# Attention and a gated convolution on one core: keys of later batches by plain loads, every eighth probability tile turned by TensorE, and a new order of the steps

## The chip, the cores and the metric

The kernel runs on one core of a Trainium2 chip. A core has five instruction streams that run beside each other: TensorE (PE in the profile, with its weight loads as PEld), VectorE (DVE), ScalarE (ACT), GpSimd (POOL) and SyncE (SP), which here only issues DMAs. Sixteen DMA engines move the data of all queues. The metric is the device time in microseconds, as the median over runs. Beside the runs there is one profiled execution, whose trace and page are read here.

## The reference

There are four batches (B = 4) with 12288 queries of 128 channels each and a key map of 384 x 32 positions. The map is averaged over 4 x 4 blocks, which leaves 768 keys per batch; keys and values are the same matrix.

```python
kv_pool = kv.reshape(B, H//4, 4, W//4, 4, C).mean(axis=(2, 4))
k = v = kv_pool.reshape(B, -1, C) @ w_sr             # 768 keys
s = (q @ k.transpose(0, 2, 1)) / sqrt(C)
a = exp(s - s.max(-1)); a /= a.sum(-1) + 1e-9
x = a @ v                                             # attention
gate_pre[t] = sum(conv_w[k] * x[t - 4 + k] for k in range(5))   # causal, by channel
out = (sigmoid(gate_pre) * (x @ w_val)) @ w_out
```

All of it is in float32. The kernel keeps that precision by splitting operands into a high and a low part.

## The kernel before

**Tiles and groups.** Queries are taken in groups of 512 (`GQ`), 24 groups per batch, 96 in all. A group has four tiles of 128 queries (`NT = 4`), and a tile is one step of the main loop (L481). So a group is four steps, j = 0 to 3.

**One tile.** TensorE makes the 128 x 768 scores in PSUM with six matmuls (`score`, L256: high times high, high times low, low times high, for two halves of the keys). VectorE takes the row maximum (`row_max`, nm), ScalarE the exponential with its row sum (`expo`, L280), in place in PSUM. ScalarE then writes the high float16 part of the probabilities (`p_hi`, L327) and VectorE the low part (`p_lo`, L331), both into the tile `hl`. Three PSUM buffers hold scores, so the scores of a tile can be made only when `p_lo` of the tile three before is done.

**Turning the probabilities.** The product with the values needs keys on the partitions. With `NX = 4`, `on_pe` is never true: each pair of tiles is turned by one DMA transpose from `hl` to `pt` (L335), two per group, issued on SP.

**One group further.** The 18 matmuls of `av_part` (L344) read all four tiles of `pt`; they are spread over the steps of the group two later, six, three, three and six (`AV_CUTS`). The row sums are inverted, turned by a small TensorE matmul (`norm_turn`, L290), stored to DRAM (`rd`) and loaded back as one row for all partitions (`rb`). VectorE multiplies av, a column scale and `rb` to x (`g_x`, L361). For the convolution GpSimd copies four columns from the x before (L357), makes four products (`tap`, L371), then four sums (L380); ScalarE makes the fifth product (L369). Then come a tanh on ScalarE, `g_val` (L400), `g_h` on VectorE (L405), `g_out` (L410), and `g_evac` (L420) to the output tile. `g_qh` (ScalarE) and `g_ql` (GpSimd, L248) split the queries of the group two ahead.

**Keys.** The first batch's keys come before the main loop in 16 pieces of 384 KB on SP (`load_kv`, L118), each summed over 4 x 4 by VectorE (L123). The keys of each later batch come during the batch before, by `setup_steps`, one entry per group: for each half of the keys one plain load (L131, SP) and three loads that add onto it as they arrive (`accum_op`, L133, on GpSimd's queue). VectorE then sums only over the remaining four neighbours, in four instructions of 768 elements per partition (L138). After that come the projection, the split and the values.

**What sets the order.** The order is written by hand (`manual_schedule`): each engine runs its instructions as the loop emits them, and waits come from the tiles. One PSUM bank (`misc`) serves `norm_turn`, `g_val`, `g_out` and the set-up matmuls in turn.

Of the kernel before, what the change touches and what calls it, by code (L numbers as in the profile page):

```python
# [27 lines left out]
def attn_moe_kernel(ctx, tc, qT, kvT, w_sr, w_moe, outT):  # L28
# [12 lines left out]
    AV_CUTS = (0, 6, 9, 12, 18)  # L41
    assert 3 * NCH == AV_CUTS[-1]
    PC = NK // PIECES
    QC = NK // 4
# [3 lines left out]
    kvp = ctx.enter_context(tc.tile_pool(name="kvp", bufs=4))  # L48
# [3 lines left out]
    pfp = ctx.enter_context(tc.tile_pool(name="pfp", bufs=3))  # L52
# [21 lines left out]
    def load_moe():  # L74
# [4 lines left out]
        raw = kvp.tile([C, HALF * R], F32, name="rows0", bufs=1).bitcast(I32)[:, :2 * NW]  # L79
        rest = kvp.tile([C, HALF * R], F32, name="rows1", bufs=1)  # L80
# [34 lines left out]
    def load_kv(st, i):  # L115
        t = kvp.tile([C, R, PC * R], F32, name="kvt", bufs=5)
        src = kvT[0].rearrange("r c x -> c r x")
        nc.sync.dma_start(out=t, in_=src[:, :, i * PC * R:(i + 1) * PC * R])  # L118
        st["kv", i] = t

    def pool_kv(st, i):
        t = st.pop(("kv", i))
        nc.vector.tensor_reduce(out=st["pool"][:, i * PC:(i + 1) * PC],  # L123
                                in_=t.rearrange("c r (k s) -> c k r s", s=R),
                                axis=AX.XY, op=ALU.add)

    def load_rows(b, st, h, r):
        src = kvT[b, r, :, h * HALF * R:(h + 1) * HALF * R]
        if r == 0:
            st["rows", h] = kvp.tile([C, HALF * R], F32, name=f"rows{h}", bufs=1)  # L130
            nc.sync.dma_start(out=st["rows", h], in_=src)  # L131
        else:
            nc.gpsimd.dma_start(out=st["rows", h], in_=src, accum_op=ALU.add)  # L133

    def pool_rows(st, i):
        t = st["rows", i // 2].rearrange("c (k s) -> c k s", s=R)
        k0 = i % 2 * QC
        nc.vector.tensor_reduce(out=st["pool"][:, i * QC:(i + 1) * QC], in_=t[:, k0:k0 + QC],  # L138
                                axis=AX.X, op=ALU.add)
# [72 lines left out]
    def value_steps(st):  # L212
        return [lambda: trickle.extend(column_scale(st)), lambda: None, lambda: None,
                lambda: values(st, 0, misc()) or split_values(st, 0),
                lambda: values(st, 1, misc()) or split_values(st, 1)]

    def setup_steps(b, st):
# [53 lines left out]
    def on_pe(j):  # L271

        return j >= NX
# [207 lines left out]
    for t in range(NT * G):  # L481
# [16 lines left out]
        if avg:  # L498
            av_part(avg, j)
# [130 lines left out]
```

## Time and profile before

| what | value |
|---|---|
| median of 3 runs | 1246.01 us (1245.61 to 1255.13) |
| profiled execution, span of its trace | 1239.7 us |
| PE, DVE, ACT, POOL busy | 1039.8, 892.6, 899.1, 878.3 us |
| weight loads (PEld) | 674.5 us |
| DMA | 253.21 MB, mean 204 GB/s |
| DMA transposes | 192, 6.1 us from issue to landing (median) |
| loads that add (GpSimd's queue) | 18 of 768 KB, 14.5 us to landing (median) |

The page gives the profiled execution's own time as its span, 1239.7 us; the median of the timed runs is 6.3 us above it. Busy shares are means over the whole span, and no engine but the DMA is above 84% by them. So the places where the engines wait, and for whom, say more than the shares.

### The profile page before, as it was taken

Reading aid. Unit: us, or ns where it says so; the run is one execution under the profiler, and the core shown is the slowest. Engines: PE = TensorE matmul, PEld = TensorE weight load, DVE = VectorE, ACT = ScalarE, POOL = GpSimd, SP = SyncE. Lnnn points to the kernel's source line nnn. Section 1 sums busy time; section 2 is a strip of 40 time slices with the busy share of each in tenths; the row PEclk is TensorE's granted clock in tenths of the full one; section 3 lists DMA queues with packets and bytes.
Section 4 is the critical chain, followed back from the end, with each engine's and each line's share of the span. In section 5 each row is a group of like instructions: output and inputs, shape, how many; then the busy total and the mean of one; then the engine's idle time right before and its main releaser. Section 6 shows DMA issues by size and latency. Waiting matters only on the chain.

```text
span 1239.7 us, 15458 instructions
## 1 busy us (share of the span) xinstructions
PE 1039.8 (84%) x4598; PEld 674.5 (54%) x4598; DVE 892.6 (72%) x1254; ACT 899.1 (73%) x1659; POOL 878.3 (71%) x966
## 2 busy tenths in 40 slices
PE   2888778699998768779999778769999999899996
PEld 1655445466565445445666545446566666566663
DVE  6966656588886657568888556557888888787784
ACT  1867666588887557668888657656888888788882
POOL 1277667678886668667888667657788888788782
PEclk9989889899999888889999988888999999999998
DMA  7799999999999999999999999999999999999994
GB/s 248 146 217 179 218 192 214 177 213 204 211 219 209 215 174 216 194 182 225 211 225 232 172 192 218 181 169 217 222 211 217 217 213 226 203 230 212 208 221 119
DMA packets 637235, 253.21 MB, mean 204 GB/s; under 512 B 600160, under 2 KB 609120, under 8 KB 637152
## 3 DMA queue, kind: packets, MB, share of 16 engines
q1 hardware_dynamic: 634560, 238.07, 94.8%
q0 software_dynamic: 2592, 14.16, 8.6%
q8 instruction: 37, 0.61, 0.2%
q14 instruction: 46, 0.38, 0.1%
HBM read 75.83 MB, written 25.36 MB: 82 GB/s over the span
## 4 chain that ended last, share of the span: by engine, by line
PE 43%; DMA 28%; DVE 13%; ACT 9%; issue 5%; POOL 1%; SPq 0%; DVEq 0%; ACTq 0%; POOLq 0%
DMA pt<-hl 23%; PE av L344 17%; PE s L262 16%; PE m L400 5%; ACT s L280 4%; DVE nm L268 4%; PE m L410 3%; DVE x L361 3%; DMA rb<-rd 3%; DVE hl L331 3%; ACT hl L327 2%; DMA kvt<-in_kv 1%; DMA q<-in_q 1%; DVE h L405 1%; ACT th L396 1%
## 5 line engine op out<-in xcount | busy, mean ns | idle before, releaser
L344 PE MATMUL av<-pt,vh 128*128 128x512 f16 x1140 | 420.2, 397 | 134.1 <-DMA pt<-hl 102.5
L280 ACT ACTIVATE s<-s,nm 128x768 f32<-128x768 f32 x384 | 335.6, 874 | 257.5 <-DVE z L287 146.4
L331 DVE SCALAR_TENSOR_TENSOR hl<-s,hl 128x768 f16<-128x768 f32 x384 | 363.0, 945 | 25.1 <-ACT hl L327 24.8
L380 POOL TENSOR_TENSOR sum<-sum,tap 128x512 f32<-128x512 f32 x282 | 359.9, 1276 | 26.4 <-ACT tap L369 4.4
L268 DVE TENSOR_REDUCE nm<-s 128x1 f32<-128x768 f32 x384 | 364.3, 949 | 2.6 <-PE s L262 2.6
L371 POOL TENSOR_SCALAR tap<-x,wm 128x512 f32<-128x512 f32 x376 | 253.6, 696 | 149.2 <-DVE x L361 146.9
L327 ACT ACTIVATE hl<-s 128x768 f16<-128x768 f32 x384 | 310.6, 809 | 18.4 <-issue 6.6
L344 PEld LDWEIGHTS <-vh 128*128 128x128 f16 x1164 | 116.5, 100 | 315.2 <-issue 192.2
L262 PE MATMUL s<-kh,qh 128*128 128x384 f32 x768 | 267.0, 430 | 21.2 <-DVE hl L331 15.5
L248 POOL TENSOR_TENSOR ql<-q,qh 128x512 fp32r<-128x512 f32 x96 | 121.6, 1267 | 163.8 <-ACT qh L244 154.1
L344 PE MATMUL av<-pt,vl 128*128 128x512 f16 x570 | 226.2, 397 | 0.0
L262 PE MATMUL s<-kl,qh 128*128 128x384 f32 x768 | 201.6, 344 | 0.0
L361 DVE SCALAR_TENSOR_TENSOR x<-av,down,rb 128x512 f32<-128x512 f32 x95 | 71.3, 751 | 180.1 <-DMA rb<-rd 89.8
L262 PE MATMUL s<-kh,ql 128*128 128x384 f32 x768 | 200.3, 342 | 0.0
L262 PEld LDWEIGHTS s<-kh,qh 128*128 128x128 f32 x768 | 142.9, 199 | 85.3 <-PE m L290 28.0
L262 PEld LDWEIGHTS s<-kl,qh 128*128 128x128 f32 x768 | 144.6, 195 | 0.5 <-DVE kl L163 0.5
L262 PEld LDWEIGHTS s<-kh,ql 128*128 128x128 f32 x768 | 143.3, 193 | 0.0
L380 POOL TENSOR_TENSOR sum<-tap,tap 128x512 f32<-128x512 f32 x94 | 119.8, 1275 | 0.0
L405 DVE SCALAR_TENSOR_TENSOR h<-th,m 128x512 f32<-128x512 f32 x94 | 64.7, 688 | 68.0 <-PE m L400 51.7
L344 PEld LDWEIGHTS <-vl 128*128 128x128 f16 x582 | 58.2, 100 | 88.4 <-issue 67.7
L400 PE MATMUL m<-x,wm 128*128 128x512 f32 x188 | 100.0, 614 | 5.5 <-DVE r L297 5.5
L410 PE MATMUL m<-h,wm 128*128 128x512 f32 x188 | 96.9, 596 | 3.9 <-DVE h L405 3.9
(62 smaller groups left out, 639.9 us busy)
## 6 DMA issues: line engine op xcount, KB each, us to landing
rb<-rd SPq DMA_DIRECT2D x96, 256.0 KB, 3.7
q<-in_q SPq DMA_DIRECT2D x47, 512.0 KB, 5.6
out<-o SPq DMA_DIRECT2D x46, 512.0 KB, 3.8
rows<-in_kv POOLq DMA_DIRECT2D x18, 768.0 KB, 14.5
kvt<-in_kv SPq DMA_DIRECT2D x16, 384.0 KB, 5.7
rows<-in_kv SPq DMA_DIRECT2D x6, 768.0 KB
pt<-hl SPq DMA_TRANSPOSE x192, 6.1
rd<-r SPq DMA_DIRECT2D x96, 2.0 KB
```

Of the source, the lines that this page charges most:

```text
L248: nc.gpsimd.tensor_tensor(out=g.ql, in0=g.q, in1=g.qh.bitcast(F32), op=ALU.subtract)
L262: nc.tensor.matmul(s[:, h, :HALF], a[:, sl], k[:, h * HALF:(h + 1) * HALF], start=(i == 0), stop=(i == 2))
L268: nc.vector.tensor_reduce(out=nm, in_=g.s[j], axis=AX.XY, op=ALU.max, negate=True)
L280: nc.scalar.activation(out=halves(g.pf[j]) if on_pe(j) else g.s[j], in_=g.s[j], func=AF.Exp, bias=g.nm.pop(j), accum_out=g.z[:, j:j + 1])
L327: nc.scalar.activation(out=part(g, j, 0), in_=g.s[j], func=AF.Copy, scale=2.0 ** 15)
L331: nc.vector.scalar_tensor_tensor(out=part(g, j, 1), in0=g.s.pop(j), scalar=2.0 ** 15, in1=part(g, j, 0), op0=ALU.mult, op1=ALU.subtract)
L344: nc.tensor.matmul(out, g.st[v][:, k * P:(k + 1) * P], g.pt[:, j0:j1, a * NCH + k], start=(i == 0), stop=(i == len(AV_ORDER) - 1))
L361: nc.vector.scalar_tensor_tensor(out=g.x[:, HALO + c0:HALO + c1], in0=av, scalar=g.st["down"], in1=g.rb[:, c0:c1], op0=ALU.mult, op1=ALU.mult)
L371: eng.tensor_scalar(out=g.tap[k], in0=src, scalar1=w, scalar2=1.0, op0=ALU.mult, op1=ALU.mult)
L380: nc.gpsimd.tensor_tensor(out=s, in0=acc, in1=g.tap[k], op=ALU.add)
L400: nc.tensor.matmul(m, wval, g.x[:, HALO + c0:HALO + c1], start=True, stop=True)
L410: nc.tensor.matmul(m, wout, h, start=True, stop=True)
```

## The change

**Keys of later batches.** The loads that add are gone. Each later batch comes in eight plain loads of 768 KB on SP, two pieces each, one in every second group (k = 1, 3, ... 15 of the batch), into three buffers. VectorE sums all 16 pieces, one per group, at step j = 1 of the groups k = 3 to 18, with the instruction that the first batch used (L123). Projection, split and values are placed at j = 1 of fixed groups (11, 19, 22, 23).

**Turning.** In every second group (odd index) the last tile, j = 3, is turned by six TensorE transposes: `expo` writes it to SBUF (`pf`), TensorE turns it back into its own PSUM buffer between the last three av matmuls, and `p_hi` and `p_lo` write it straight into `pt`. Its neighbour j = 2 goes alone through a DMA transpose of half the size. All other tiles go as before.

**Order.** x, with the convolution behind it, moves from the end of j = 3 to the end of j = 0 of the next group; the last sum of the convolution moves behind ScalarE's product at j = 1. `g_out` and `g_evac` move to j = 0 one group later, `g_val` to j = 2, `g_h` to j = 3. `norm_turn` uses spare columns of a score buffer instead of the `misc` bank. `g_qh` and `g_ql` move to j = 3. The av matmuls are spread three, six, three, six. Queries are loaded four groups ahead (three buffers) instead of two.

**Beginning and end.** The first batch's keys come in two single pieces, six double pieces and two single pieces, three loads ahead; the first queries are split late in that phase; the last weights are loaded after it. The tail is rearranged to fit.

```diff
-    AV_CUTS = (0, 6, 9, 12, 18)
+    AV_CUTS = (0, 3, 9, 12, 18)
...
-    def load_rows(b, st, h, r):
-        src = kvT[b, r, :, h * HALF * R:(h + 1) * HALF * R]
-        if r == 0:
-            st["rows", h] = kvp.tile([C, HALF * R], F32, name=f"rows{h}", bufs=1)
-            nc.sync.dma_start(out=st["rows", h], in_=src)
-        else:
-            nc.gpsimd.dma_start(out=st["rows", h], in_=src, accum_op=ALU.add)
...
+    def load_kv(b, st, i, n=2):
+        t = kvp.tile([C, R, 2 * PC * R], F32, name="kvt")[:, :, :n * PC * R]
+        src = kvT[b].rearrange("r c x -> c r x")
+        nc.sync.dma_start(out=t, in_=src[:, :, i * PC * R:(i + n) * PC * R])
...
+    def setup_step(k, b, st):
+        if k == 1:
+            key_tiles(st)
+        if k < PIECES and k % 2 == 1:
+            load_kv(b, st, k - 1)
+        if 3 <= k < 3 + PIECES:
+            pool_kv(st, k - 3)
+        if k == 20:
+            trickle.extend(column_scale(st))
...
-    def on_pe(j):
-        return j >= NX
+    def on_pe(g, j):
+        return g.i % 2 == 1 and j == NT - 1
...
+    def turn(g, j, k):
+        c = k % (NCH // 2) * P
+        nc.tensor.transpose(g.s[j][:, k // (NCH // 2), c:c + P],
+                            g.pf[j][:, k * P:(k + 1) * P], ident)
...
-        if j % 2:
-            j0 = j - 1
+        if on_pe(g, j):
+            return
+        if j % 2 or on_pe(g, j + 1):
+            j0 = j - j % 2
             nc.sync.dma_start_transpose(
...
         if nxt:
             score(nxt, (j + 1) % NT)
-        if mg and j == 1:
+        if last and j == 1:
+            norm_turn(last, nxt.spare)
+        if og and j == 0:
+            og.m = g_out(og.h, misc())
...
+        if avg:
+            av_slice(avg, lo, mid)
+        if mg and j == 2:
             mg.m = g_val(mg, misc())
...
+        if turned:
+            for i in range(NCH):
+                turn(cur, j, i)
+                if avg and mid + i < hi:
+                    av_slice(avg, mid + i, mid + i + 1)
+            cur.pf.pop(j)
+        else:
+            p_hi(cur, j)
...
+        if turned:
+            p_hi(cur, j)
         if prev:
             p_lo(prev, (j - 1) % NT)
...
-        if avg and j == 3:
-            new_x(avg, xg, nc.gpsimd.tensor_copy)
-            g_x(avg, avg.av)
-        if xg and j == 1:
-            g_conv(xg)
+        if xg and j == 0:
+            new_x(xg, mg, nc.gpsimd.tensor_copy)
+            g_x(xg, xg.av)
+            g_conv(xg)
+        if mg and j == 3:
+            mg.h = g_h(mg.th, mg.m)
+        if ahead is not None and j == 1:
+            setup_step(k, cur.b + 1, ahead)
```

**TensorE, at the end of step j = 3 of a group, and of an odd group now.** Before, the last four of that step's six av matmuls, with their weight loads, are followed by the next tile's scores (s).

```order
L344 LDWEIGHTS vh
L344 MATMUL av<-pt,vh 128x512
L344 LDWEIGHTS vh
L344 MATMUL av<-pt,vh 128x512
L344 LDWEIGHTS vl
L344 MATMUL av<-pt,vl 128x512
L344 LDWEIGHTS vh
L344 MATMUL av<-pt,vh 128x512
L262 MATMUL s<-kh,qh 128x384 x2
```

Now the last three av matmuls alternate with the transposes of `pf` (L302), and three more transposes stand ahead of the next scores.

```order
L302 MATMUL s<-ident,pf 128x128
L338 LDWEIGHTS vh
L338 MATMUL av<-pt,vh 128x512
L302 MATMUL s<-ident,pf 128x128
L338 LDWEIGHTS vl
L338 MATMUL av<-pt,vl 128x512
L302 MATMUL s<-ident,pf 128x128
L338 LDWEIGHTS vh
L338 MATMUL av<-pt,vh 128x512
L302 MATMUL s<-ident,pf 128x128 x3
L256 MATMUL s<-kh,qh 128x384 x2
```

So the first transpose waits for ScalarE's exponential of that tile, and three av matmuls and the next scores stand behind it on TensorE.

**VectorE, one group in the main loop, from x to the step before the next x.** Before, nm is the row maximum, hl the low part, r the turned row sums, h the gated values.

```order
L361 SCALAR_TENSOR_TENSOR x<-av,down,rb 128x512
L268 TENSOR_REDUCE nm<-s 128x1
L287 RECIPROCAL z_102<-z_102 128x4
L331 SCALAR_TENSOR_TENSOR hl<-s,hl 128x768
L268 TENSOR_REDUCE nm<-s 128x1
L297 COPY r<-m 4x128
L331 SCALAR_TENSOR_TENSOR hl<-s,hl 128x768
L405 SCALAR_TENSOR_TENSOR h<-th,m 128x512
L268 TENSOR_REDUCE nm<-s 128x1
L331 SCALAR_TENSOR_TENSOR hl<-s,hl 128x768
L268 TENSOR_REDUCE nm<-s 128x1
L331 SCALAR_TENSOR_TENSOR hl<-s,hl 128x768
```

Now a group with a piece of keys to sum (pool from kvt) stands so.

```order
L355 SCALAR_TENSOR_TENSOR x<-av,down,rb 128x512
L263 TENSOR_REDUCE nm<-s 128x1
L323 SCALAR_TENSOR_TENSOR hl<-s,hl 128x768
L123 TENSOR_REDUCE pool<-kvt 128x48
L292 COPY r<-s 4x128
L263 TENSOR_REDUCE nm<-s 128x1
L323 SCALAR_TENSOR_TENSOR hl<-s,hl 128x768
L263 TENSOR_REDUCE nm<-s 128x1
L323 SCALAR_TENSOR_TENSOR hl<-s,hl 128x768
L404 SCALAR_TENSOR_TENSOR h<-th,m 128x512
L263 TENSOR_REDUCE nm<-s 128x1
L282 RECIPROCAL z_102<-z_102 128x4
```

The reciprocal and one low part now stand ahead of x, h stands two tiles later, and the sum over keys stands behind the first low part, with the copy of r behind it.

**SP, two groups while keys of the next batch arrive.** Before, the loads that add are on GpSimd's queue and SP has four transposes of 24 blocks in two groups.

```order
L298 DMA rd<-r 4x128
L335 DMA_TRANSPOSE pt<-hl 128x24x128
L303 DMA rb<-rd 128x512
L335 DMA_TRANSPOSE pt<-hl 128x24x128
L298 DMA rd<-r 4x128
L335 DMA_TRANSPOSE pt<-hl 128x24x128
L303 DMA rb<-rd 128x512
L233 DMA q<-in_q 128x1024
L335 DMA_TRANSPOSE pt<-hl 128x24x128
L424 DMA out<-o 128x1024
```

Now one of the four transposes has 12 blocks, and the load of keys stands among them.

```order
L293 DMA rd<-r 4x128
L329 DMA_TRANSPOSE pt<-hl 128x24x128
L298 DMA rb<-rd 128x512
L329 DMA_TRANSPOSE pt<-hl 128x24x128
L118 DMA kvt<-in_kv 128x4x384
L293 DMA rd<-r 4x128
L329 DMA_TRANSPOSE pt<-hl 128x24x128
L329 DMA_TRANSPOSE pt<-hl 128x12x128
L298 DMA rb<-rd 128x512
L227 DMA q<-in_q 128x1024
```

The key load stands ahead of the odd group's row sums and transposes, and the half transpose follows the whole one directly.

More of the change, by code (lines that the diff above doesn't have):

```diff
@@ L264, in score @@
         g.s[j] = s[:, :, :HALF]
+        g.spare = s[:, 0, HALF:]
     def row_max(g, j):
@@ L372, in tap, with add_taps @@
                               op0=ALU.mult, op1=ALU.mult)
+    def add_taps(g, acc, k):
+        s = work.tile([C, GQ], F32, name=f"sum{1 - k % 2}", bufs=1 if k % 2 else 2)
+        nc.gpsimd.tensor_tensor(out=s, in0=acc, in1=g.tap[k], op=ALU.add)
+        return s
     def g_conv(g):
@@ L376, in g_conv, with g_conv_last @@
             tap(g, k, nc.gpsimd)
-        acc = g.tap[0]
-        for i, k in enumerate(range(1, TAPS)):
-            s = work.tile([C, GQ], F32, name=f"sum{i % 2}", bufs=1 + i % 2)
-            nc.gpsimd.tensor_tensor(out=s, in0=acc, in1=g.tap[k], op=ALU.add)
-            acc = s
-        g.gate = acc
+        g.gate = g.tap[0]
+        for k in range(1, TAPS - 1):
+            g.gate = add_taps(g, g.gate, k)
+    def g_conv_last(g):
+        g.gate = add_taps(g, g.gate, TAPS - 1)
     def conv_dve(g, c0=0, c1=GQ):
@@ L492, in attn_moe_kernel @@
         if nxt:
             score(nxt, (j + 1) % NT)
-        if mg and j == 1:
-            mg.m = g_val(mg, misc())
+        if last and j == 1:
+            norm_turn(last, nxt.spare)
+        if og and j == 0:
+            og.m = g_out(og.h, misc())
+        if gi == 1 and j in (0, 1):
+            values(st, j, misc())
+            high, low = split_values(st, j)
+        if ahead is not None and j == 1 and k > 1:
+            high, low = setup_matmul(k, ahead)
+        turned = on_pe(cur, j)
@@ new lines, in attn_moe_kernel @@
+        lo, hi = AV_CUTS[j], AV_CUTS[j + 1]
+        mid = lo + 3 if turned else hi
+        if avg:
+            av_slice(avg, lo, mid)
+        if mg and j == 2:
+            mg.m = g_val(mg, misc())
+        if last and j == 2:
+            norm_store(last)
+        row_max(cur, j)
+        if last and j == 0:
+            norm_reciprocal(last)
+        expo(cur, j)
+        if turned:
[4 more added lines that the diff above has]
+            cur.pf.pop(j)
+        else:
+            p_hi(cur, j)
@@ L496, in attn_moe_kernel @@
+        if j == NT - 1:
+            norm_eps(cur)
+            if at(gi + 2):
+                g_qh(at(gi + 2))
+        if og and j == 0:
+            out_tile(og)
+            g_evac(og, og.m)
+        if xg and j == 1:
+            tap(xg, TAPS - 1, nc.scalar)
+            g_conv_last(xg)
         if mg and j == 2:
-            mg.m = g_out(mg.h, misc())
-        if avg:
-            av_part(avg, j)
-        if high and (j == 0 or t < NT):
+            mg.th = g_tanh(mg.gate)
+        if high:
@@ L556, in attn_moe_kernel @@
     p_lo(n1, NT - 1)
+    n5.m = g_out(n5.h, misc())
+    norm_turn(n1, bank())
+    out_tile(n5)
+    g_evac(n5, n5.m)
     store_pair(n5)
-    norm_turn(n1, misc())
+    new_x(n3, n4, nc.scalar.copy)
+    g_x(n3, n3.av)
+    av_slice(n2, 0, 9)
+    norm_store(n1)
+    norm_rows(n1)
+    g_conv(n3)
+    tap(n3, TAPS - 1, nc.scalar)
+    g_conv_last(n3)
     n4.th = g_tanh(n4.gate)
-    norm_store(n1)
     n4.m = g_val(n4, misc())
-    av_part(n2, 0)
-    norm_rows(n1)
-    tap(n3, TAPS - 1, nc.scalar)
-    g_conv(n3)
+    av_slice(n2, 9, 18)
     h = g_h(n4.th, n4.m)
-    for i in (1, 2, 3):
-        av_part(n2, i)
     new_x(n2, n3, nc.scalar.copy)
```

143 lines of the change are left out of this document (52 added, 91 removed).

## The prediction

> **What bounds the kernel now.** I read the page first, then the waits, then windows by stage, then the chain of waits in a quiet stretch. The page's DMA queues (packets, MB, share of 16 engines) and four rows of the waits (total us, times, longest):
>
> ```profile
> span 1239.7 us, 15458 instructions
> q1 hardware_dynamic: 634560, 238.07, 94.8%
> q0 software_dynamic: 2592, 14.16, 8.6%
> PE av L344 <- DMA pt<-hl: 102.5, 26, 10.1
> PEld L344 <- DMA pt<-hl: 39.5, 13, 9.5
> DVE x L361 <- DMA rb<-rd: 89.8, 14, 9.3
> ACT qh L244 <- DMA q<-in_q: 18.4, 11, 8.6
> ```
>
> The DMA engines are as good as full, and TensorE and VectorE each stand for about 100 us behind transposes and behind `rb`. The windows (us, then busy time of PE, PEld, DVE, ACT, POOL, clock, DMA share, GB/s) say where. Keys of the next batch arrive in 98:240, 400:560 and 700:870.
>
> ```profile
> core 0: us, PE busy (x) PEld busy (x) DVE busy (x) ACT busy (x) POOL busy (x), PEclk, DMA share, GB/s
> 58.00:98.00 40.00, 32.07 (x142) 21.07 (x140) 27.14 (x39) 26.80 (x51) 29.22 (x33) 0.91 1.03 216
> 98.00:240.00 142.00, 110.44 (x470) 71.82 (x470) 88.17 (x121) 92.55 (x171) 95.90 (x106) 0.89 1.07 195
> 240.00:364.00 124.00, 117.22 (x528) 75.60 (x529) 100.73 (x143) 103.32 (x192) 99.55 (x109) 0.97 1.05 211
> 364.00:400.00 36.00, 31.15 (x139) 20.18 (x138) 26.35 (x36) 26.84 (x49) 27.30 (x30) 0.95 1.09 215
> 400.00:560.00 160.00, 120.04 (x517) 77.44 (x516) 97.32 (x133) 101.32 (x188) 104.40 (x116) 0.89 1.09 196
> 672.00:700.00 28.00, 24.40 (x107) 15.99 (x107) 20.42 (x29) 20.37 (x38) 21.12 (x24) 0.94 1.02 233
> 700.00:870.00 170.00, 129.88 (x548) 84.25 (x548) 103.43 (x141) 107.90 (x198) 110.85 (x122) 0.88 1.09 189
> 870.00:982.00 112.00, 106.38 (x494) 69.04 (x493) 93.08 (x134) 96.23 (x181) 92.45 (x102) 1.00 1.06 217
> 982.00:1195.00 213.00, 199.59 (x918) 130.91 (x917) 172.20 (x237) 180.09 (x331) 178.70 (x196) 0.99 1.04 215
> ```
>
> PE's instruction count measures the work done. The quietest stretch, 870:982, takes 112/494 = 0.2267 us per PE instruction, with the clock at 1.00. By that pace 98:240 should take 470 x 0.2267 = 106.6 us; it takes 142, a loss of 35.4. Likewise 400:560 loses 42.8 and 700:870 45.8. That is 124 us in the three stretches with keys in flight. 58:98, 364:400 and 672:700, where those loads begin, lose 7.8 + 4.5 + 3.7 = 16. 240:364 and 982:1195 lose 4.3 + 4.9 = 9. All losses: 149 us.
>
> What sets the quiet pace is seen in one group of the chain (start, us, what) and in GpSimd's timeline (the last bracket is idle time and its releaser):
>
> ```profile
> 1002.85 0.75 DVE x L361
> ...
> 1004.55 0.85 DVE hl L331
> 1005.40 0.14 issue
> 1005.54 1.28 PE s L262 x6
> 1006.81 0.86 PE m L400 x2
> 1007.67 0.65 PE av L344 x3
> 1008.32 1.04 PE s L262 x6
> 1009.36 0.86 PE m L410 x2
> ...
> 1011.91 1.33 PE av L344 x6
> ...
> 1013.33 0.75 DVE x L361
> ```
>
> ```profile
> 1003.77 2.69 POOL L371 TENSOR_SCALAR tap<-x,wm 128x512 f32<-128x512 f32 x4 [0.88 <-DVE x L361]
> 1013.06 0.19 POOL L357 COPY x<-x 128x4 f32<-128x4 f32 x1
> 1014.25 2.70 POOL L371 TENSOR_SCALAR tap<-x,wm 128x512 f32<-128x512 f32 x4 [1.01 <-DVE x L361]
> ```
>
> From x to x is 10.48 us, and GpSimd's taps repeat at 10.48 as well. GpSimd has nothing idle but the 1.0 us in which VectorE, having waited for GpSimd's copy, makes x. So a quiet group is a GpSimd loop of 9.5 + 1.0 us. PE's own work in it is four scores at 1.04, two products at 0.86, 18 av matmuls at 0.65 per three, and a small transpose of 0.11 (the first row below): 4.16 + 1.72 + 3.90 + 0.11 = 9.89, which leaves 0.59 us per group.
>
> **The change part by part.** Rows that price it, in turn: a transpose in the chain at 609.74, the same as a group, a sum of keys, SP's time on a DMA transpose (min/median/max ns), the first 28 us, in which the first batch's keys are loaded plainly, and an accumulating load's issue on GpSimd:
>
> ```profile
> 609.74 0.11 PE m L290
> L290 PE MATMUL m<-ident,z 128*128 128x128 f32 x96 | 29.3, 306 | 2.6 <-DVE vl L205 1.5 <-DVE z L287 1.1
> L123 DVE TENSOR_REDUCE pool<-kvt 128x48 f32<-128x768 f32 x16 | 15.2, 952 | 7.6 <-DMA kvt<-in_kv 7.4
> L335 SPq DMA_TRANSPOSE pt<-hl x192: 3579/4340/12493, 36.7 to 1213.0; - x192
> 0.00:28.00 28.00, 3.62 (x5) 1.34 (x5) 17.65 (x28) 3.19 (x6) 1.96 (x7) 1.00 0.88 274
> L133 POOL DMA_DIRECT2D rows<-in_kv x18 | 16.0, 888 | 0.0
> ```
>
> *Key loads.* The accumulating queue takes 8.6% of 1239.7, 106.6 us of all 16 engines, for 14.16 MB. Plain loads reach 274 GB/s at a share of 0.88, 311 GB/s at a full share: 14.16 MB then cost 45.5 us. That frees 61 us, 20 per batch, all in the stretches that lose.
>
> *Transposes.* 48 of 192 halve: 24 whole ones, at 3.58 to 4.34 us each, free 86 to 104 us, 9 to 11 in each stretch of about ten groups.
>
> *The two together.* 98:240 holds 142 x 1.07 = 152 us of DMA time; after, 152 - 20 - 10 = 122. A quiet stretch carries 1.06 x 112/494 = 0.240 per PE instruction, 113 for 470. So keys would come within 8% of the quiet load. The new order adds room: av of a group still starts a group after its last transpose, now behind a `g_out` more (0.86 us) and with half as many matmuls at once; in odd groups the last transpose is half and a step earlier; x is a step further behind `rb`; queries are loaded two groups earlier. I let 130 of the 140 us in the key stretches and their beginnings go, and the 9 elsewhere. Bounds: nothing left, or 33 to 61 left (first rival).
>
> *Cost on SP.* Each key load (768 KB, 2.5 us at 311 GB/s) now stands ahead of `rd` and the transposes of its odd group. They have most of a group until av, so nothing; if that cover is gone, 24 loads x 2.5 = 60, the same money as the first rival's.
>
> *Sums on VectorE.* 48 instead of 12: 36 x 0.952 = 34 us. VectorE is busy 93.08 of 112 us in the quiet stretch, so a group has 10.48 x 0.17 = 1.8 us idle for one sum of 0.95. The sum also adds a wait for the load, issued two groups earlier; the copy of r, the next maximum and low part queue behind it. Bounds 0 and 34; nearer 0: 5.
>
> *Turning.* Six transposes are 6 x 0.11 = 0.66 us of PE per two groups, against 2 x 0.59 idle: hidden. By the group's mean, 6 x 0.306 = 1.84, it would expose 0.66 x 48 = 32. The row at 609.74 is the pipelined case, and here av matmuls stand between: 5 us, for the wait on the exponential too.
>
> *Order.* GpSimd's instructions and the loop copy, x, taps stay, so the group is not under 10.48. The quiet stretch's pace is 10.65 for a group's 47 PE instructions (24 scores, 18 av, 4, 1) because the `misc` bank is shared with set-up; with `norm_turn` out of it, 0 to 0.17 x 94 groups = 16 comes back: 8. The 18 issues on GpSimd (16 us) are inside the 124.
>
> *Beginning and end.* x comes a step later (+2.6, a quarter of a group); one `g_out` moves into the tail (+0.9); 6.29 MB at 311 GB/s would take 20 instead of about 25 us (-5). Zero, bounds -5 to +4.
>
> *Sum.* 1239.7 - 149 + 10 + 5 + 5 - 8 = 1103 for the span. The median of the timed runs lies 6.3 above this span: **1109**.
>
> **The rivals.** *The DMA stays the bound.* Bytes do not change. If a share of 1.06 is the ceiling, 122/1.06 = 115 us against 106.6: 8.5 of 35.4, 24% of the 140, stay, 33; if 1.00 is, 15.4 of 35.4, or 61. Against my 10 that is 23 to 51 more: 1132 to 1160. For it speaks that share; against it, that quiet stretches run well at 1.06, so that the figure contains waiting. The Trainium skill, page "DMA: Bandwidth & Descriptors", section "Issuing engines are not separate DMA queues", says that DMAs of all queues run on the same 16 engines, so a move from one queue to another saves issue time only. By that rule the loads would give back GpSimd's 16 us of issue at most; the trace disagrees in part, since 14.16 MB took 8.6% where the plain price makes it 3.7%.
>
> *VectorE becomes the bound* where keys are summed: all 34 us show, 1138. For it: x already waits for GpSimd, and a late low part holds TensorE's next scores. Against: 1.8 us idle per group.
>
> *The turned tile stops TensorE (slower).* The first transpose waits for that tile's exponential, and av and the next scores stand behind it. If the round trip is exposed, it costs, by these rows, exponential 0.874 + 0.197, transposes 0.66, high part 0.809, low part 0.945: 3.5 us.
>
> ```profile
> L280 ACT ACTIVATE s<-s,nm 128x768 f32<-128x768 f32 x384 | 335.6, 874 | 257.5 <-DVE z L287 146.4 <-PE s L262 97.6 <-DVE nm L268 12.8
> L280 ACT ACTIVATION_READ_ACCUMULATOR s<-s,nm 128x1 f32 x384 | 75.5, 197 | 0.0
> L327 ACT ACTIVATE hl<-s 128x768 f16<-128x768 f32 x384 | 310.6, 809 | 18.4 <-issue 6.6 <-DMA pt<-hl 2.6 <-ACT s L280 0.2
> L331 DVE SCALAR_TENSOR_TENSOR hl<-s,hl 128x768 f16<-128x768 f32 x384 | 363.0, 945 | 25.1 <-ACT hl L327 24.8 <-DVE r L297 0.3
> ```
>
> 48 x 3.5 = 168, less the 5 I count: 1109 + 163 = 1272. It decides from (1258 - 1104)/48 = 3.2 us per turned tile, where 1258 is 1% over the median. Against it: the tile's scores end 0.65 + 0.86 (av, `g_val`) + 1.04 + 0.65 = 3.2 us before PE reaches the transpose; the maximum, a reduction of as many elements as a sum of keys (0.95), and the exponential (1.07) need 2.0. The Trainium skill, page "TensorE: Matmul & The Clock Gate", section "Part 2: What happens when you issue a matmul", says that matmuls keep program order and only weight loads are pulled ahead. By that rule nothing passes a waiting transpose; no run here shows one yet.
>
> *The change does not do what it says*: the half transpose takes as long as a whole one and plain keys cost what adding ones did. Then the losses stay: 1239.7 + 5 + 5 + 6.3 = 1256.
>
> **How the numbers follow.** Forecast 0.60, DMA 0.20, VectorE 0.11, turned tile 0.05, nothing gained 0.04. About 1% is what a measurement of this kernel can tell from no change. Faster by more: 0.60 + 0.20 + 0.11 = 0.91; within: 0.04; slower: 0.05. The low end is the forecast with every gain: 1239.7 - 149 - 16 - 5 + 6.3 = 1076, say 1075. The high end takes in VectorE's rival and the DMA's with the end's 4: 1165. What lies above is the last two cases and their mixtures, under 2 in 10.
>
> **What would show it.** The groups should come every 10.5 to 10.8 us also while keys arrive; PE's and PEld's waits for pt, 142 us now, should fall under 30, and x's wait for `rb` to almost nothing. q0 should be empty. x should wait for GpSimd's copy, and GpSimd be over 80% busy. PE should wait under 0.5 us for a turned tile's exponential. I am wrong if key stretches still take over 12 us a group with PE waiting for pt; if VectorE has no idle time there; or if a turned step stands out by 3 us.

## The result and the profile after

The changed kernel takes 1110.18 us (median of four runs, 1107.44 to 1111.28), the kernel before 1245.81 us beside it (four runs, 1233.85 to 1255.13). The ratio is 0.8959, with a 95% interval of 0.8909 to 0.901. The profiled execution of the changed kernel took 1109.72 us, and its trace has a span of 1107.9 us. Runs over 1.5% slower than the fastest of the same kernel are left out of the comparisons below.

The page of the kernel after begins so (share of the span behind the busy time, then instructions), and this is its one large DMA queue:

```profile
span 1107.9 us, 16093 instructions
...
PE 1019.8 (92%) x4886; PEld 695.0 (63%) x4886; DVE 918.8 (83%) x1290; ACT 902.1 (81%) x1660; POOL 865.2 (78%) x947
...
q1 hardware_dynamic: 569472, 233.35, 97.8%
```

TensorE is busy for 92% of the span, before for 84%. GpSimd's queue q0 is gone from the page. The DMA engines are still 97.8% full, yet the waits of the kernel after (total us, times, longest) show that in the main loop hardly anything waits for them any more:

```profile
POOL tap L365 <- DVE x L355: 109.1, 56, 3.0
...
DVE pt L323 <- ACT pt L319: 79.8, 48, 2.0
...
ACT pt L319 <- PE s L302: 67.2, 48, 1.7
PE av L338 <- DVE x L355: 38.6, 57, 1.6
...
PEld s L302 <- ACT pf L275: 9.2, 12, 0.9
...
PE s L302 <- ACT pf L275: 3.5, 9, 0.4
...
DVE x L355 <- DMA rb<-rd: 2.3, 3, 1.4
...
DVE x L355 <- POOL x L351: 1.1, 1, 1.1
...
PEld L338 <- DMA pt<-hl: 0.6, 1, 0.6
```

The two rows that stood for 142 us of TensorE's waits for `pt` are down to 0.6 us, and x's wait for `rb` from 89.8 to 2.3. What is left are the waits of the new turned tile: ScalarE for the transposes, VectorE for ScalarE, and TensorE's first av matmul of a group for x. (Ahead of the main loop, VectorE still waits 10.6 us for the first batch's keys.)

The windows of the kernel after, cut at the first x, at every 24th x behind it and, for the last batch, short of the tail, have these columns: window, its length, PE, PEld, DVE, ACT, POOL, granted clock, DMA share, GB/s.

```profile
65.00:327.00 262.00, 249.16 (x1208) 170.55 (x1209) 224.81 (x314) 223.62 (x412) 220.10 (x241) 1.00 1.03 220
327.00:593.00 266.00, 252.79 (x1219) 172.04 (x1218) 225.66 (x316) 225.40 (x416) 220.62 (x241) 1.00 1.03 221
593.00:856.00 263.00, 251.89 (x1217) 171.74 (x1216) 225.31 (x314) 224.60 (x414) 220.01 (x241) 1.00 1.03 221
856.00:1074.00 218.00, 211.53 (x1026) 145.53 (x1025) 179.33 (x247) 189.67 (x348) 186.69 (x206) 1.00 0.96 200
```

The clock is 1.00 in all four; before it was 0.88 to 0.89 where keys arrived. There TensorE was busy for longer per instruction as well: 110.44 / 470 = 0.235 us in 98:240, against 106.38 / 494 = 0.215 in the quiet 870:982. Over the three stretches with keys that makes 30 of the 124 us. Whether the lower clock was a cause of the loss or only came with the waits was not tried.

The best measure of the pace is the time from one x to the next. It is worked out here from the starts of x on VectorE, of which the trace has one per group:

```
us from x to x               before    after    difference
start of the span to x 1       57.8     65.1       +7.3
24 groups, batch 0            306.3    262.0      -44.3
24 groups, batch 1            307.8    265.8      -42.0
24 groups, batch 2            310.0    263.2      -46.8
22 groups, batch 3            236.8    229.8       -7.0
from there to the end          21.0     22.0       +1.0
```

The sum is -131.8, which is the difference of the two spans. The last batch, which loads no keys, gains only 7.0. So nearly all of the gain is where keys arrive, and the beginning gives 7 us back. The chain of waits holds only 2% of the span here, so the timeline stands in its place. VectorE first, in a group with keys and then in a quiet one of the last batch (start, us, instruction, idle time before it and who ended it):

```profile
106.58 0.74 DVE L355 SCALAR_TENSOR_TENSOR x<-av,down,rb 128x512 f32<-128x512 f32 x1
...
108.97 0.94 DVE L123 TENSOR_REDUCE pool<-kvt 128x48 f32<-128x768 f32 x1
...
117.41 0.96 DVE L323 SCALAR_TENSOR_TENSOR pt<-s,pt 128x768 f16<-128x768 f32 x1 [1.77 <-ACT pt L319]
118.28 0.74 DVE L355 SCALAR_TENSOR_TENSOR x<-av,down,rb 128x512 f32<-128x512 f32 x1
...
930.92 0.96 DVE L323 SCALAR_TENSOR_TENSOR pt<-s,pt 128x768 f16<-128x768 f32 x1 [1.77 <-ACT pt L319]
931.79 0.74 DVE L355 SCALAR_TENSOR_TENSOR x<-av,down,rb 128x512 f32<-128x512 f32 x1
...
941.28 0.74 DVE L355 SCALAR_TENSOR_TENSOR x<-av,down,rb 128x512 f32<-128x512 f32 x1
```

With keys and a sum (`pool`) the odd group takes 118.28 - 106.58 = 11.70 us; groups alternate 11.7 and 9.6. In the quiet stretch they alternate 11.8 and 9.5, and 941.28 - 931.79 = 9.49 is one of the short ones. Both make 21.3 per pair. So by pairs a group with keys costs what a quiet one costs, and the sum leaves no trace in the pace. What is above 10.65 per group in the three batches, 6.4 + 10.2 + 7.6 = 24 us, sits mostly in the groups with the set-up matmuls (14.1 and 13.2 us at the two projections).

TensorE and ScalarE at that quiet turned tile:

```profile
928.57 0.27 PE L302 MATMUL s<-ident,pf 128*128 128x128 f32 x1
928.68 0.38 PE L338 MATMUL av<-pt,vh 128*128 128x512 f16 x1
...
929.55 0.49 PE L302 MATMUL s<-ident,pf 128*128 128x128 f32 x3
930.07 0.81 ACT L319 ACTIVATE pt<-s 128x768 f16<-128x768 f32 x1 [1.65 <-PE s L302]
930.92 1.02 PE L409 MATMUL m<-h,wm 128*128 128x512 f32 x2
932.58 0.38 PE L338 MATMUL av<-pt,vh 128*128 128x512 f16 x1 [0.65 <-DVE x L355]
```

TensorE does not wait for the exponential at all here; a transpose takes 0.11 us of its stream (928.57 to 928.68). ScalarE and VectorE wait for each other in turn. x stands behind the turned tile's low part, and av has one PSUM bank, so the first av matmul of the next group waits 0.65 us for x. That is the only idle time that TensorE shows in this pair. GpSimd's taps in the same pair:

```profile
932.71 2.71 POOL L365 TENSOR_SCALAR tap<-x,wm 128x512 f32<-128x512 f32 x4 [2.40 <-DVE x L355]
...
942.22 2.70 POOL L365 TENSOR_SCALAR tap<-x,wm 128x512 f32<-128x512 f32 x4
```

They are 9.51 us apart in the short group with nothing idle ahead of the second, and GpSimd has waited 2.40 us for x in the long one.

### The profile page after: what moved, and what is told of

It is laid out like the page before. It is cut to its first block, busy times and chain, and to the rows that moved or that the text cites. A ratio compares the mean times of both kernels' runs of the same rounds, so it can differ in the third digit from the quotient of the medians.

```text
span 1107.9 us, 16093 instructions
## 1 busy us (share of the span) xinstructions
PE 1019.8 (92%) x4886; PEld 695.0 (63%) x4886; DVE 918.8 (83%) x1290; ACT 902.1 (81%) x1660; POOL 865.2 (78%) x947
## 3 DMA queue, kind: packets, MB, share of 16 engines
q1 hardware_dynamic: 569472, 233.35, 97.8%
## 5 line engine op out<-in xcount | busy, mean ns | idle before, releaser
L338 PE MATMUL av<-pt,vh 128*128 128x512 f16 x1140 | 408.4, 381 | 38.6 <-DVE x L355 38.6
L275 ACT ACTIVATE s<-s,nm 128x768 f32<-128x768 f32 x336 | 293.5, 874 | 71.0 <-DVE nm L263 68.5
L323 DVE SCALAR_TENSOR_TENSOR hl<-s,hl 128x768 f16<-128x768 f32 x336 | 316.6, 942 | 8.8 <-ACT hl L319 8.8
L256 PE MATMUL s<-kh,qh 128*128 128x384 f32 x768 | 280.7, 446 | 10.6 <-DVE hl L323 8.7
L319 ACT ACTIVATE hl<-s 128x768 f16<-128x768 f32 x336 | 272.5, 811 | 10.7 <-DMA pt<-hl 0.2
L338 PE MATMUL av<-pt,vl 128*128 128x512 f16 x570 | 216.0, 379 | 0.0
L256 PE MATMUL s<-kl,qh 128*128 128x384 f32 x768 | 197.6, 338 | 0.0
L256 PEld LDWEIGHTS s<-kl,qh 128*128 128x128 f32 x768 | 139.9, 189 | 0.5 <-DVE kl L149 0.5
L323 DVE SCALAR_TENSOR_TENSOR pt<-s,pt 128x768 f16<-128x768 f32 x48 | 46.0, 957 | 79.8 <-ACT pt L319 79.8
L319 ACT ACTIVATE pt<-s 128x768 f16<-128x768 f32 x48 | 38.9, 811 | 67.2 <-PE s L302 67.2
```

The costliest lines, as they stand in the source:

```text
L256: nc.tensor.matmul(s[:, h, :HALF], a[:, sl], k[:, h * HALF:(h + 1) * HALF], start=(i == 0), stop=(i == 2))
L275: nc.scalar.activation(out=halves(g.pf[j]) if on_pe(g, j) else g.s[j], in_=g.s[j], func=AF.Exp, bias=g.nm.pop(j), accum_out=g.z[:, j:j + 1])
L319: nc.scalar.activation(out=part(g, j, 0), in_=g.s[j], func=AF.Copy, scale=2.0 ** 15)
L323: nc.vector.scalar_tensor_tensor(out=part(g, j, 1), in0=g.s.pop(j), scalar=2.0 ** 15, in1=part(g, j, 0), op0=ALU.mult, op1=ALU.subtract)
L338: nc.tensor.matmul(out, g.st[v][:, k * P:(k + 1) * P], g.pt[:, j0:j1, a * NCH + k], start=(i == 0), stop=(i == len(AV_ORDER) - 1))
```

## The experiments

**Which part brings it.** The change was cut into three: the keys (plain or adding), the turned tile, and the new order with its beginning and end. All combinations were run, each with the kernel before beside it (its medians lie between 1233.6 and 1246.92 us; gains below are against the one beside). Beside the turned tile in the old order, the doubled sums, the additional turned tiles and the plain loads on GpSimd's queue the kernel before scattered most, from 1227.34 to 1258.44, so these four ratios are the least sure.

*Old order, plain keys.* To before, in the set-up of a batch:

```diff
-        for h, r in loads:
-            steps += [lambda: None, lambda h=h, r=r: load_rows(b, st, h, r)]
-        steps += [lambda i=i: (None, lambda: pool_rows(st, i)) for i in range(4)]
+        def entry(n):
+            ...
+            if n < PIECES and n % 2 == 0:
+                load_two(b, st, n)
+            return (None, lambda: pool_kv(st, n - 1)) if n else None
```

> The kernel before with plain key loads of 768 KB on SP and 16 sums, one a group, in place of the loads that add; order, transposes and beginning as before. Theory A: the accumulating queue's 61 us of extra DMA time is what overloads the key stretches, so two thirds of the 140 us lost there go: 1140 to 1165 us. Theory B: the order (av and x close behind their transposes and rb) is what makes a full DMA late, so plain keys alone give little: 1200 us or more. Theory C: all of it goes: 1095 to 1120 us.

1189.01 us (1185.68 to 1189.64), ratio 0.9531 (0.9509 to 0.9553). That is between the first two expectations, and the DMA still makes engines late: TensorE waits 86.7 + 40.6 = 127 us for `pt`, ScalarE 44.1 us for queries.

*Old order, turned tile.* To before:

```diff
-    def on_pe(j):
-        return j >= NX
+    def on_pe(g, j):
+        return g.i % 2 == 1 and j == NT - 1
...
-        if j % 2:
-            j0 = j - 1
+        if on_pe(g, j):
+            return
+        if j % 2 or on_pe(g, j + 1):
+            j0 = j - j % 2
```

Here the six transposes stand in one block behind the av matmuls of the step, not between them.

> The kernel before with the last tile of every second group turned by TensorE, and nothing else changed. Theory A (the DMA is what overloads, so 24 transposes less pay wherever they are taken away): the 86 to 104 us of DMA time freed give 30 to 60 us: 1185 to 1215 us. Theory B (with loads that add, freed DMA time gives nothing, as the changed order with such loads gave nothing): 1235 to 1260 us, with the turned tile's 0.66 us and a wait of VectorE for its high part added.

1180.3 us (1179.04 to 1183.01), ratio 0.9554 (0.9482 to 0.9625): a little better than the first expectation. The freed DMA time need not be all of it. In the kernel before, eleven of the 18 adding loads were issued 0.15 to 0.4 us behind a transpose; here each has its next transpose 1.9 us behind it, and GpSimd's queue takes 6.2% of 1178.3 us, 73 us, instead of 107. The two were not separated.

*Old order, both.* The two edits above together.

> The kernel before with plain key loads and with turned tiles, in the old order: all of the change but its order and beginning. Theory A (keys and turning both only free DMA time, and together they free enough): the key stretches come down to the old order's quiet pace of 10.5 to 11.3 us a group: 1115 to 1140 us, so that the order is worth 5 to 30 us of it. Theory B (the old order holds av and x so close behind their transfers that a busy DMA still makes them late): 1150 us or more.

1150.07 us (1147.7 to 1154.01), ratio 0.9258 (0.9207 to 0.9309). Here each group with a sum takes at least 11.3 us from x to x, a quiet one 10.5 to 10.6. So in the old order a sum does cost about 0.75 us on the path, 48 x 0.75 = 36 in all. In the new order it costs nothing that shows. The time meets the second expectation, at its edge. ScalarE still waits 59.0 us for queries here, in 37 places, against 3.4 us in the kernel after, which loads them two groups earlier. Which part of the order brings its 40 us was not tried further.

*New order without the turned tile.* To after:

```diff
     def on_pe(g, j):
-        return g.i % 2 == 1 and j == NT - 1
+        return False
```

> The changed kernel without turned tiles: all 192 transposes whole and on the DMA. Theory A: if plain keys and the new order alone make the DMA fit, TensorE loses 48 x 0.66 us of transposes and the 38.6 us wait behind them: 1035 to 1060 us. Theory B: the half transposes are what makes it fit; without them key stretches take 11 to 12 us a group again and TensorE waits for pt by 50 us or more: 1110 to 1160 us.

1170.2 us (1163.26 to 1171.68), ratio 0.9377 (0.9346 to 0.9408). Its waits, and the queue on its page:

```profile
PE av L338 <- DMA pt<-hl: 94.9, 44, 4.8
...
PEld L338 <- DMA pt<-hl: 56.6, 26, 4.5
...
DVE x L355 <- DMA rb<-rd: 8.3, 10, 2.7
```

```profile
q1 hardware_dynamic: 643200, 252.23, 102.5%
```

With all 192 transposes whole, the DMA is the bound again: TensorE waits over 150 us for `pt`, as the second expectation had it, and the time is above its range. At a share of 102.5% it waits, at 97.8% in the kernel after it doesn't.

*New order with adding loads and the turned tile; and without the turned tile.* To after, the keys as before (the second kernel has `return False` in `on_pe` as well):

```diff
-        if k < PIECES and k % 2 == 1:
-            load_kv(b, st, k - 1)
-        if 3 <= k < 3 + PIECES:
-            pool_kv(st, k - 3)
+            load_rows(b, st, 0, 0)
+            load_rows(b, st, 1, 0)
+        if 3 <= k <= 13 and k % 2 == 1:
+            n = (k - 3) // 2
+            load_rows(b, st, n % 2, 1 + n // 2)
+        if 15 <= k < 19:
+            pool_rows(st, k - 15)
...
-        for h, at_k in enumerate((11, 19)):
+        for h, at_k in enumerate((18, 19)):
```

> The changed kernel with the later keys by loads that add on GpSimd's queue and four sums per batch, as before; order, turning and beginning as changed. Theory A: keys come back at 61 us more of DMA time and the key stretches lose again, against room made by 24 fewer transposes: 1135 to 1175 us. Theory B: order and turning alone made the room: 1100 to 1125 us. Theory C: the key loads were all of it: 1220 us or more.

> The changed kernel's order and beginning with the old data movement: loads that add, and every tile by DMA transposes. Theory A (the new order's room makes late transposes cheaper): 1180 to 1235 us. Theory B (the order gives nothing while keys arrive by adding, as with turned tiles, where 1247 us was measured): 1240 to 1300 us.

With the turned tile: a median of 1247.09 us, widely scattered. The fastest run took 1204.91, the other three 1241.74 to 1270.87, so the comparison rests on one run, which fits none of the three expectations. Without: 1196.96 us (1187.46 to 1203.04), ratio 0.9607 (0.9522 to 0.9691), as the first expectation of this run had it. Turning, a gain of 53 us in the old order and of 60 in the new order with plain keys (1170.2 to 1110.18), gains nothing in this company. It is taken up below.

```
us                       old order  new order
adding, no turned tile       1242       1197
plain, no turned tile        1189       1170
adding, turned tile          1180       1205 (one run)
plain, turned tile           1150       1110
```

The parts do not add up: alone, keys, turned tile and order are worth 58, 53 and 45 us, 156 together, and all three give 135.

**What sets the pace now.** *x ahead of the turned tile's low part.* To after, at the end of a step:

```diff
+        if xg and j == 0:
+            new_x(xg, mg, nc.gpsimd.tensor_copy)
+            g_x(xg, xg.av)
+            g_conv(xg)
         if prev:
             p_lo(prev, (j - 1) % NT)
         if low:
             low()
             low = None
-        if xg and j == 0:
-            new_x(xg, mg, nc.gpsimd.tensor_copy)
-            g_x(xg, xg.av)
-            g_conv(xg)
```

> The changed kernel with x moved ahead of the low part of the tile before, at j = 0. Theory A: TensorE sets the pace of the changed kernel, and its only wait is the first av matmul of a group, which cannot overwrite the av bank until VectorE has made x, which stands behind the turned tile's low part (38.6 us in all). Then that wait goes and the time falls by 25 to 40 us, to 1070 to 1085 us, with two groups taking 20.5 to 20.8 us. Theory B, the prediction's: a loop through GpSimd (copy, x, taps) sets the pace. Then nothing changes: 1105 to 1115 us. Theory C: the low part, now 0.7 us later, holds the next scores as much as it saves: 1100 to 1115 us with the wait moved to the scores.

1095.75 us (1091.73 to 1098.12), ratio 0.8787 (0.8762 to 0.8812): between the first two expectations. Quiet groups now take 10.2 us each without alternation. That is TensorE's own work, (2 x 9.89 + 0.66) / 2 = 10.22, and in 870:1060 of this trace TensorE is busy for 190.00 of 190.00 us, so TensorE bounds them, and GpSimd can go faster than 10.48. The gain is only 14.5 us, because with keys the groups vary from 9.9 to 14.2. Its waits, and the queue on its page, say why:

```profile
DVE x L355 <- DMA rb<-rd: 26.0, 15, 4.0
...
PE av L338 <- DVE x L355: 15.8, 12, 3.0
```

```profile
q1 hardware_dynamic: 569472, 233.35, 101.0%
```

At the quicker pace the DMA comes next: `rb` is late 15 times, and av waits for that x.

*The same, with more tiles turned while keys arrive.*

```diff
     def on_pe(g, j):
-        return g.i % 2 == 1 and j == NT - 1
+        keys = g.b < B - 1 and 2 <= g.i % NG < 19
+        return j == NT - 1 and (g.i % 2 == 1 or keys)
```

> The kernel with x ahead of the low part, and with the last tile of every group turned while keys of the next batch arrive (24 tiles more). Theory A: there the DMA, not TensorE, sets the pace of the kernel with x first (its groups vary from 9.9 to 14 us, 10.9 on the mean, against 10.2 without keys), so 12 transposes less pay more than 24 x 0.66 us of TensorE cost: 1070 to 1090 us. Theory B: the turned tile itself is what spreads those groups: 1095 to 1115 us.

1088.42 us (1087.91 to 1088.73), ratio 0.8807 (0.8744 to 0.887), as the first expectation had it. Groups with keys take a flat 10.6 us (12.6 and 13.5 at the two projections), x no longer waits for `rb`, and the queue on its page is less full:

```profile
q1 hardware_dynamic: 528000, 222.74, 96.5%
```

This version beats both kernels; against the kernel after it is 21.8 us. That last step confirms the cause of the one before: with fewer transposes the bumps are gone. The flat 10.6 is near 9.89 + 0.66 = 10.55, TensorE's own work with a turned tile in every group.

*Every sum of keys made twice.*

```diff
         if 3 <= k < 3 + PIECES:
+            st["again"] = st["kv", k - 3]
+            pool_kv(st, k - 3)
+            st["kv", k - 3] = st["again"]
             pool_kv(st, k - 3)
```

> The changed kernel with each of the 48 later sums over keys made twice, to the same place. If VectorE's added sums are hidden, as the equal pace of groups with and without them says, another 48 x 0.944 = 45 us of VectorE stays mostly hidden too: 1110 to 1122 us. If they lie on the path: 1145 to 1158 us.

1141.13 us (1139.33 to 1142.54), ratio 0.9233 (0.9165 to 0.9301): 31 us more than after, between the two expectations. 48 further sums of 0.948 are 45 us of VectorE. Groups with keys went from 11.7 and 9.6 to 12.0 and 10.6. So the short group had no room for a second sum and the long one had most of it: the first 48 sums were free, and they used up much of what VectorE had. The next kernel makes no sum in most of the groups that load keys, and there the pace is the same 11.8 and 9.5.

**What the adding loads cost.** *The keys on GpSimd's queue as before, same bytes, but without adding.* To the kernel with adding loads and the turned tile; the sum over four rows is left out, so keys of the later batches are other ones:

```diff
-            nc.gpsimd.dma_start(out=st["rows", h], in_=src, accum_op=ALU.add)
+            nc.gpsimd.dma_start(out=st["rows", h], in_=src)
```

> The changed kernel with the later keys loaded on GpSimd's queue as in the kernel with loads that add, with the same bytes, sizes and waits, but without the adding: each of the three loads overwrites (the sum of four rows is left out, so the keys of batches 1 to 3 are other ones). Theory A: adding is what costs; then the queue's share falls from 8.3% to 3 to 4% and the time to 1105 to 1135 us. Theory B: the queue of GpSimd costs, whatever it carries: share 7 to 8%, 1200 us or more.

1118.76 us (median of three runs, 1117.48 to 1130.43; a fourth took 1136.88), ratio 0.9095 (0.8919 to 0.9271). The queue's rows on the two pages, first with adding (span 1240.0), then without (span 1117.0):

```profile
q0 software_dynamic: 2592, 14.16, 8.3%
```

```profile
q0 software_dynamic: 2592, 14.16, 4.6%
```

8.3% of 1240.0 is 103 us, 4.6% of 1117.0 is 51, a little over the 3 to 4% that were expected. In the other kernels with adding loads the row gives 73 us (6.2% of 1178.3, old order with the turned tile), 86 (7.2% of 1201.0, new order alone) and 107 (8.6% of 1239.7, before); in the two that follow it gives 112 (8.5% of 1314.9) and 82 (7.0% of 1165.9). So adding makes the same bytes 1.4 to 2.2 times as dear, depending on the kernel. Shares above 100%, as on the page of the kernel with x first, show that such rows count waiting too. The queue itself costs little: 9 us against plain loads on SP (1110.18), which lie in one batch of the trace (274.3 us against 265.8; the other two differ by 0.3). The Trainium skill, page "DMA: Bandwidth & Descriptors", section "Issuing engines are not separate DMA queues", says that DMAs of every queue run on the same 16 engines and that another issuing engine saves issue time only. By that rule the move of plain loads from one queue to the other should hardly show, and the trace agrees within these 9 us. The 8.6% of the queue before, by which the prediction saw a disagreement, belongs to the adding, not to the queue.

*The adding loads issued a group earlier*, in even groups, against the idea that they meet the two directly following transposes of odd groups:

```diff
-        if 3 <= k <= 13 and k % 2 == 1:
-            n = (k - 3) // 2
+        if 2 <= k <= 12 and k % 2 == 0:
+            n = (k - 2) // 2
```

> The changed kernel with loads that add (the one measured at 1247 us), but each adding load issued one group earlier, in the even groups, which have no half transpose. Theory A: the loss there is a meeting of place: the adding load is issued beside the odd group's whole and half transposes, rb stands behind both on SP, and x behind rb; one group earlier it goes: 1150 to 1200 us. Theory B: adding loads cost the same wherever they are issued: 1230 to 1260 us.

A median of 1318.87 us; the fastest run took 1279.15, the other three 1316.64 to 1324.46. That is worse than either expectation, and by the fastest runs too (1279.15 against 1204.91) the loads in even groups lose, so the idea of the odd groups is refuted. This kernel's issues (KB each, median us to landing) and timeline:

```profile
kvt<-in_kv POOLq DMA_DIRECT2D x18, 768.0 KB, 22.3
```

```profile
748.23 26.68 SPq L347 DMA_TRANSPOSE pt<-hl  x1
748.87 0.89 POOL L133 DMA_DIRECT2D kvt<-in_kv  x1
```

One whole transpose held SP for 26.68 us, where 4.3 is usual; it was issued 0.6 us ahead of an adding load. This trace is of a run of 1316.64 us, and that of the new order with adding loads and the turned tile of one of 1241.74. Their fastest runs have no trace, so how often a transpose is held in those is not known.

*`rb` ahead of the transposes in odd groups.* To the new order with adding loads and the turned tile:

```diff
+        if last and j == 2 and cur.i % 2:
+            norm_rows(last)
         if prev:
             p_lo(prev, (j - 1) % NT)
...
-        if last and j == 3:
+        if last and j == 3 and not cur.i % 2:
             norm_rows(last)
```

> The kernel with the new order, turned tiles and adding loads, but in odd groups the load of rb stands on SP ahead of the whole and the half transpose of that step instead of behind both. There the slow version had SP held 26.48 us by two transposes beside an adding load, with rb behind them, groups of 21 to 28 us, and x waiting 118 us for rb. Theory A (rb behind two held transposes is what made turning a loss in that company): x's wait for rb falls under 30 us, the groups with adding loads to 12 to 17 us as in the new order alone, and the median to 1165 to 1200. Theory B (the transposes themselves come too late for the av matmuls, wherever rb stands): TensorE's waits for pt take the place of x's wait for rb, groups of over 20 us stay, and the median is 1215 to 1270.

1164.6 us (1156.13 to 1167.69), ratio 0.9379 (0.93 to 0.9458). The groups over 20 us are gone; the worst are 18.6. The timelines of the kernel without and with this edit, around an adding load:

```profile
719.91 26.48 SPq L347 DMA_TRANSPOSE pt<-hl  x2
719.93 0.89 POOL L133 DMA_DIRECT2D kvt<-in_kv  x1
746.49 0.54 SPq L316 DMA_DIRECT2D rb<-rd  x1
```

```profile
706.42 0.89 POOL L133 DMA_DIRECT2D kvt<-in_kv  x1
709.26 0.43 SPq L311 DMA_DIRECT2D rd<-r  x1
715.03 0.33 SPq L316 DMA_DIRECT2D rb<-rd  x1
715.47 6.00 SPq L347 DMA_TRANSPOSE pt<-hl  x2
```

The time lies at the edge of the first expectation, but the trace shows more than a new order on SP. x no longer waits for `rb`, and TensorE's waits for `pt` are 50.3 + 16.0 us, so the second expectation's wait is there in part. And the transposes themselves are no longer held: none takes over 9.8 us. `rb` waits for `rd` to be written, and in all cases but the first the pair starts 1.7 us or more behind the load.

In the kernel without the edit, the 18 pairs of transposes issued nearest to an adding load divide so: nine were issued from 0.08 us ahead of it to 0.14 behind it and took 9.9 to 26.5 us; the other nine, 0.16 us or more away, took at most 9.6. In the kernel with loads in even groups, eleven transposes issued from 0.8 us ahead of an adding load to 0.12 us behind it took 19 to 27 us, and of the others none took over 15.5. With plain loads on the same queue, the six pairs issued within 0.7 us of a load took 6.0 to 13.4 us. So holds of 16 us and more are seen only beside loads that add.

But meeting such a load is not enough. In the kernel before, eleven transposes issued 0.15 to 0.4 us ahead of an adding load took only 4.2 to 8.1 us. What else it takes is open. That the held transposes are why turning gains nothing in this company fits the traces; it is not shown, since the edit changes the place of `rb` and the meeting together, and the fastest run without the edit has no trace. Against the kernel after, the adding loads still cost 54 us in this form.

## Why the prediction was right, and where not

The forecast was 1109 us, 1075 to 1165, faster by over 1% with a chance of 0.91. It came out at 1110.18. For the span the sum gave 1103, the trace 1107.9. The 6.3 us between span and median before were added to the forecast; after, they are 2.3. So a span that was 4.9 too low and an offset that was 4.0 too high make up for each other, and a miss of 1 us is luck. Term by term:

- **The losses of 149 us with 10 left over.** Right. The four batches became 44.3 + 42.0 + 46.8 + 7.0 = 140.1 us shorter, where the terms inside them make -149 + 10 + 5 + 5 - 8 = -137. The place was right as well: 133 of it in the three batches that load keys. The means were as stated, DMA time freed by both parts: without the turned tile 60 us come back, with waits for `pt`, and with adding loads at least 54. By the queue rows the DMA time fell from 103.4% of 1239.7 to 97.8% of 1107.9, by 198 us, where the terms freed 61 and 86 to 104.
- **The quiet pace as a GpSimd loop that no group can be under.** Wrong for the new order. Even groups take 9.5 us, x waited for GpSimd's copy once (1.1 us) and GpSimd is busy for 78%, not over 80%. Carrying the loop over from the old order was the failing step ("GpSimd's instructions and the loop copy, x, taps stay"). In the kernels with the old order, quiet groups do stay at 10.5 with the turned tile too. In the new one TensorE's 20.4 us per pair and the wait of av for x make the pace, 21.3 per pair against 2 x 10.48. The run with x first shows it.
- **Sums, 5 us.** The forecast's choice near nothing held: groups with a sum are not longer. But the room was smaller than its 1.8 us per group minus one sum suggests, as the doubled sums show, and the rival's 34 us are real in the old order (36 us by the groups of 11.3). It is the new order that hides them; the sum gave that no term. Which part of the order does it was not tried.
- **Turning, 5 us.** Mis-sized. The exponential cost 9.2 + 3.5 = 12.7 us of waiting in 48 tiles, 0.26 each, as the text would have it. The cost that the text missed goes another way: ScalarE waits 67.2 us for the transposes, VectorE 79.8 us for ScalarE, x is late by that and av by x, 38.6 us on TensorE. Some of it takes the place of idle time that was there before; a quiet pair is 21.3 - 20.96 = 0.3 us longer, 16 us over 47 pairs.
- **The `misc` bank, -8 us.** Not found. The set-up groups still stand out, by 24 us over three batches. What they wait for was not tried.
- **Beginning and end, 0 with bounds -5 to +4.** Outside its bounds: +7.3 and +1.0. The first row maximum starts at 31.59 instead of 30.47, so the re-cut loads gained nothing. The rest fits the step by which x is later (2.6 us in the prediction) and waits in the first groups, though the two were not separated. VectorE's timeline of after has three such waits ahead of the first x:

```profile
43.11 0.56 DVE L191 TENSOR_TENSOR vl<-m,vh 128x384 f16<-128x384 f32 x1 [1.41 <-ACT vh L188]
47.21 0.56 DVE L191 TENSOR_TENSOR vl<-m,vh 128x384 f16<-128x384 f32 x1 [1.41 <-ACT vh L188]
55.13 0.96 DVE L323 SCALAR_TENSOR_TENSOR pt<-s,pt 128x768 f16<-128x768 f32 x1 [1.14 <-ACT pt L319]
```

So the sum is nearer than its terms deserve. Beginning and end missed 8 us, turning 11 and the bank 8. Against them stand the 5 us kept for the sums and, by subtraction, some 17 more than expected where keys arrive.

The rivals: **the DMA stays the bound** did not happen, though its share is 97.8%; it would have without the turned tile (1170.2, past its 1132 to 1160), and it is what stops the version with x first. Its "bytes do not change" was wrong: the half transposes move less, and the two queues carry 233.35 MB instead of 252.23. **VectorE becomes the bound**: its price shows in the old order and with doubled sums, not in this kernel. **The turned tile stops TensorE** is refuted: no round trip of 3.5 us shows. The Trainium skill, page "TensorE: Matmul & The Clock Gate", section "Part 2: What happens when you issue a matmul", says that matmuls stay in program order. By that rule a late exponential holds everything behind it; the trace keeps that order at 928.57 to 929.55, and the wait was 0.26 us per turned tile, since the exponential is done in time. **Plain keys cost what adding ones did** is refuted by the queue's shares, and its other half by the half transposes: a pair of a whole and a half takes SP 5.7 us, one whole 4.3.

## What to carry to other kernels

Where the DMA engines are full, price a DMA by what it takes of them, not by its bytes: adding loads took 1.4 to 2.2 times the time of plain ones, and one slab of transposes moved to TensorE freed more than it cost there. When the pace of a loop is put down to one engine, ask whether the new order keeps that loop; an engine that looked like the floor in the old order had 10% to spare in the new one. Measure the parts in both orders: the turned tile alone gained 53 us in the old order and nothing in the new one, until the keys were loaded plainly.

## What was not expected of the hardware

- Adding loads took 73 to 112 us of the DMA engines' time, by kernel, where plain loads of the same bytes on the same queue took 51.
- In two kernels, DMA transposes issued at nearly the same moment as an adding load took 9.9 to 26.7 us, where one takes 4.3 and a pair of a whole and a half 5.7. Pairs issued 1.7 us or more behind the load took at most 9.8 in a third. In the kernel before, transposes 0.15 to 0.4 us ahead of the load took only 4.2 to 8.1, and those 2.7 to 8.4 us behind it 6.2 to 12.5.
- The DMA share tells little near the top. In the new order, at 97.8% hardly anything waited, at 101.0% x waited 26 us for `rb`, and at 102.5% TensorE waited over 150 us for `pt`. In the old order ScalarE waited 91.1 us for queries at 97.0% (turned tile alone) and 59.0 at 98.1% (with plain keys).
